# Strassen's scheme for layer 1's last two blocks, and layer 2's weights by way of DRAM scratch

## The chip, the core and the metric

The kernel runs on one core of one Trainium2 chip. The metric is the device time of one execution in microseconds (us); before the change it is 572.56 us, the median of three runs. Five engines work side by side, each through its own instructions in order: TensorE (PE in the profile), VectorE (DVE), ScalarE (ACT), GpSimd (POOL) and SyncE (SP), which issues the DMAs. Between engines there are only semaphores, so an instruction that waits holds up everything behind it on its engine.

## What is computed

A linear-attention pass over 4 batches, 8 heads and 768 positions gives `attn_out`; it is laid out as 3072 tokens of 256 features and goes through two layers of the same shape, all in float32:

```python
x = np.ascontiguousarray(attn_out.transpose(0, 2, 1, 3)).reshape(B * S, H * D)   # 3072 x 256
h = x @ w_in                       # layer 1: 256 -> 2048
g = np.maximum(h, 0.0) + np.log1p(np.exp(-np.abs(h)))
x = (g @ w_out)                    # 2048 -> 256
h = x @ w2_in                      # layer 2
g = np.where(h >= 1, h, np.where(h <= -1, 0.0, (h + 1) ** 2 / 4))
return (g @ w2_out)
```

## The kernel before

The tokens are cut into six blocks of 512 (`c`, 0 to 5), the 2048 features into 16 columns of 128 (`fc`). One **step** is one block and one column in one layer `m`: `up` makes h (128 x 512) in a PSUM bank, an activation makes g, and `down` adds g times the column's rows of `w_out` to the block's two accumulators (`acc`). Float32 products are made of three matmuls: every operand is split into a high part that the matmul takes exactly and a low part that is the rest (`xh`/`xl`, `wih`/`wil`, `woh`/`wol`, `gh`/`gl`), and high x high, high x low and low x high are added. An `up` is 6 matmuls of 512 columns, a `down` 6 too (4 with gh, 2 with gl).

In layer 2 `up` is made by Strassen's scheme: two blocks and two columns form a **quad** of four steps. Instead of 8 products of 3 matmuls it takes 7, of sums of weight pieces (S, made by `s_sum`, `s_hi`, `s_lo`) and sums of token pieces (T, made by `t_sum`, `t_hi`, `t_lo`). On PE a quad is `p15`, `p26`, `p37`, `p4`; between them ACT copies two banks (`fork`, `keep`) and DVE adds twice (`add1`, behind the second product of `p26` and ahead of `p37`; `add2`, behind `p37` and ahead of `p4`). PE fills the gaps with `down` matmuls of earlier steps.

Weights come from HBM as 64-bit numbers. `load_w` brings one eighth of a matrix, `w0` to `w3` turn it into float32 (ACT and DVE), `w_hi` and `split_w` split it. Layer 1's weights are made while the attention of the first blocks runs. Layer 2's take the same SBUF tiles, so each waits for the last use of layer 1's piece (`last_use`); they are made between 230 and 320 us, in three temporaries (`w32`).

The attention of block c, in units of 128 positions per batch, runs between layer 1's steps: loads of `ld`, `u` and `bc` (SP), `decay` scans, `sources`, `weigh` (DVE), `scores`, `st`, `out` (PE), `evac` (ACT) and `ready` (DVE), the last of which gives the block's `xl`.

The order of all this is not written by hand. `program()` lists jobs with engine, cost, needs, buffers taken and given, and due time; `Jobs.order` places them greedily by start time and due time, and the instructions are emitted in that order. `CHUNK` sets how early attention falls due, `LAG` and `LAG_2` how far `down` may follow `up`, `T_POOL` which T sums go to POOL, `STRETCH` how long PE's steps are taken to be.

Of the kernel before, what the change touches and what calls it, by code (L numbers as in the profile page):

```python
# [156 lines left out]
def mlp_steps():  # L157
# [9 lines left out]
    pairs = [(0, NC // 2 - 1)] + [(1, p) for p in range(NC // 2)]  # L167
    steps += [(m, c, 0, T, i, 1) for m, p in pairs for i in range(NFC) for c in (2 * p, 2 * p + 1)]
# [3 lines left out]
def quad_of(s):  # L172

    return s // 4 if s >= NFC * NC else None
# [32 lines left out]
def program():  # L207
# [116 lines left out]
    last_use, first_use = {}, {}  # L324
    for s, (m, c, t0, n, fc, m_fc) in enumerate(steps):
        for j in {(fc + i) // 2 for i in range(m_fc)}:
            last_use[m, "i", j] = ("up", s)
            last_use[m, "o", j] = ("down", s)
            first_use.setdefault((m, j), s)
    for m in range(2):  # L330
        for j in sorted(range(8), key=lambda j: first_use[m, j]):
            for kind in "io":
                w = (m, kind, j)
                add(("load_w", *w), SP, 400, takes=["sx" if m == 0 and j == SX else "st" if m else ("st", "st3")], size=524e3)
                add(
                    ("w0", *w), {ACT: 580} if signed(*w) else {ACT: 580, DVE: 350}, needs=[("load_w", *w)] + [("ready", NU - 1)] * m, takes=["w32"] * m,
                )
                if m < LOW_ACT:
                    add(("w1", *w), ACT, 680, needs=[("load_w", *w)], takes=[("t", "g")])
# [16 lines left out]
    for p in range(NC // 2):
        done = [("finish_lo", 0, c, e) for c in (2 * p, 2 * p + 1) for e in range(2)]
        first = NFC * NC // 4
        late = [[("ready", NU - 1)], [("w3", 1, kind, 7) for kind in "io"] + [("p4", first + 3)], [("p4", first + 9)]][p]
        t = [("t_sum", p, i) for i in range(4)]  # L360
# [137 lines left out]
def tile_kernel(ctx: ExitStack, tc: tile.TileContext, a0, al, bc, ub, w_in, w_out, w2_in, w2_out, out):  # L498
# [894 lines left out]
```

## Time and profile before

| | |
|---|---|
| median of three runs | 572.56 us (572.38 to 572.74) |
| the profiled execution | 571.61 us |
| its span (first to last instruction) | 569.7 us |
| PE busy | 560.1 us (98%) |
| DVE busy | 440.3 us (77%) |
| ACT busy | 335.0 us (59%) |
| POOL busy | 42.3 us (7%) |
| DMA, mean | 68 GB/s |
| granted clock of PE | 0.999 |

The profile is of one execution. Busy is the time in which an engine had an instruction of its own at work. Matmuls overlap in the records: a row says 0.39 us for one, while the next starts 0.227 us later, so times on PE are read from starts. A row's brackets show how long the engine was idle before it and whose signal ended that. A line such as L1176 is a line of the kernel above.

### The profile page before, as it was taken

The numbers are of one execution on the slowest core, as the hardware profiler recorded it, in microseconds if no ns is written. First come the engines' busy times: TensorE is split into PE (matmuls) and PEld (weight loads), VectorE is DVE, ScalarE is ACT, GpSimd is POOL, SyncE is SP. The second block draws the span as 40 slices with busy tenths as digits, with TensorE's granted clock in tenths as the row PEclk, the third lists the DMA queues.
The fourth block names the chain that finished last, engine by engine and source line by source line (L and its number), as shares of the span: only waits on it lengthen the run. The fifth ranks groups of instructions, "written<-read, shape, count | busy, mean of one in ns | idle before, by whom it ended". The sixth has DMA issues, their size and how long they took to land.

```text
span 569.7 us, 10297 instructions
## 1 busy us (share of the span) xinstructions
PE 560.1 (98%) x4103; PEld 450.9 (79%) x4103; DVE 440.3 (77%) x807; ACT 335.0 (59%) x601; POOL 42.3 (7%) x43
## 2 busy tenths in 40 slices
PE   8899999999999999999999999999999999999997
PEld 3778798877877777888888788888887888788885
DVE  7999987647547754799999888977798776876674
ACT  6969343324324322666655877675686764777863
POOL 5230000000000600200020000200021000000000
PEclk9999999999999999999999999999999999999999
DMA  8984653313312200114241000000100000100001
GB/s 275 372 247 156 191 136 105 93 29 104 93 30 75 75 1 2 27 48 145 78 148 37 1 0 1 1 2 0 75 0 2 1 1 37 38 0 2 1 1 74
DMA packets 19988, 38.49 MB, mean 68 GB/s; under 512 B 2052, under 2 KB 2436, under 8 KB 19940
## 3 DMA queue, kind: packets, MB, share of 16 engines
q1 hardware_dynamic: 19940, 37.84, 21.4%
q8 instruction: 32, 0.52, 0.4%
q14 instruction: 16, 0.13, 0.1%
HBM read 34.50 MB, written 3.33 MB: 66 GB/s over the span
## 4 chain that ended last, share of the span: by engine, by line
PE 93%; DVE 2%; DMA 1%; ACT 1%; issue 1%; SPq 1%; DVEq 0%; ACTq 0%
PE acc L1262 44%; PE h L1126 6%; PE h L1127 6%; PE h L1128 6%; PE h L1133 3%; PE h L1135 3%; PE h L1134 3%; PE z L1133 3%; PE z L1135 3%; PE z L1134 3%; PE acc L1250 2%; PE y L1036 1%; DMA st<-in_w_in_dram 1%; PE z L1126 1%; PE z L1127 1%; PE z L1128 1%
## 5 line engine op out<-in xcount | busy, mean ns | idle before, releaser
L1236 DVE TENSOR_TENSOR gl<-g,gh 128x512 fp32r<-128x512 f32 x186 | 130.7, 705 | 36.3 <-PE acc L1262 21.2
L1262 PE MATMUL acc<-gh,woh 128*128 128x512 f32 (+1 forms) x384 | 149.5, 391 | 0.0
L1262 PE MATMUL acc<-gh,wol 128*128 128x512 f32 (+1 forms) x384 | 146.3, 383 | 0.0
L1262 PE MATMUL acc<-gl,woh 128*128 128x512 f32 (+1 forms) x384 | 115.2, 383 | 0.6 <-DVE gl L1236 0.6
L1221 ACT ACTIVATE g<-h 128x512 f32<-128x512 f32 x74 | 44.1, 596 | 105.7 <-PE h L1128 105.0
L623 DVE CAST gh<-g 128x512 fp32r<-128x512 f32 x93 | 42.5, 459 | 55.6 <-ACT g L1221 51.1
L1262 PEld LDWEIGHTS acc<-gh,woh 128*128 128x128 f32 x384 | 72.1, 188 | 16.8 <-issue 1.7
L1262 PEld LDWEIGHTS acc<-gl,woh 128*128 128x128 f32 x384 | 70.8, 188 | 15.3 <-DVE gl L1236 1.0
L1262 PEld LDWEIGHTS acc<-gh,wol 128*128 128x128 f32 x384 | 72.2, 188 | 13.3
L621 ACT CAST gh<-g 128x512 fp32r<-128x512 f32 x93 | 57.7, 620 | 30.9 <-PE acc L1262 20.2
L1126 PE MATMUL h<-xh,wih 128*128 128x512 f32 (+1 forms) x180 | 67.6, 376 | 0.0
L1127 PE MATMUL h<-xh,wil 128*128 128x512 f32 (+1 forms) x180 | 65.9, 366 | 0.0
L1128 PE MATMUL h<-xl,wih 128*128 128x512 f32 (+1 forms) x180 | 65.8, 365 | 0.0
L1213 ACT ACTIVATE t<-t 128x512 f32<-128x512 f32 x96 | 60.8, 634 | 2.2
L1126 PEld LDWEIGHTS h<-xh,wih 128*128 128x128 f32 x180 | 33.9, 188 | 6.2 <-issue 0.5
L1127 PEld LDWEIGHTS h<-xh,wil 128*128 128x128 f32 x180 | 33.9, 189 | 6.0 <-issue 0.5
L1128 PEld LDWEIGHTS h<-xl,wih 128*128 128x128 f32 x180 | 33.9, 188 | 5.7
L1206 ACT ACTIVATE t<-h 128x512 f32<-128x512 f32 x37 | 22.1, 597 | 14.7 <-PE h L1135 11.4
L932 DVE TENSOR_TENSOR_SCAN ld<-ld,eye_t 128x512 f32<-128x512 f32 x20 | 25.7, 1318 | 1.7 <-DMA ld<-clip_z 1.7
L1206 ACT ACTIVATE t<-z 128x512 f32<-128x512 f32 x35 | 20.8, 595 | 9.9 <-PE z L1135 7.7
L1225 DVE TENSOR_TENSOR g<-h,t 128x512 f32<-128x512 f32 x37 | 25.4, 685 | 1.2 <-DVE gl L1236 0.5
L1225 DVE TENSOR_TENSOR g<-z,t 128x512 f32<-128x512 f32 x35 | 23.9, 686 | 0.6
(337 smaller groups left out, 884.7 us busy)
## 6 DMA issues: line engine op xcount, KB each, us to landing
st<-in_w_in_dram SPq DMA_DIRECT2D x15, 512.0 KB, 4.1
st<-in_w_out_dram SPq DMA_DIRECT2D x15, 512.0 KB, 4.3
u<-in_ub_dram SPq DMA_DIRECT2D x24, 256.0 KB, 5.2
ld<-clip_z SPq DMA_DIRECT2D x20, 256.0 KB, 4.4
bc<-in_bc_dram SPq DMA_DIRECT2D x12, 384.0 KB, 3.5
out_dram<-st_plain SPq DMA_DIRECT2D x6, 256.0 KB, 2.0
dec<-clip_p SPq DMA_DIRECT2D x5, 256.0 KB
out_dram<-dec_plain SPq DMA_DIRECT2D x4, 256.0 KB, 2.2
```

The lines of the kernel that those rows point to most:

```text
L621: nc.scalar.copy(out, in_)
L623: engines[engine].tensor_copy(out, in_)
L1126: nc.tensor.matmul(o, wh, xh[c][:, k, t0:t0 + n], start=(k == 0), stop=False)
L1127: nc.tensor.matmul(o, wl, xh[c][:, k, t0:t0 + n], start=False, stop=False)
L1128: nc.tensor.matmul(o, wh, xl[c][:, k, t0:t0 + n], start=False, stop=(k == 1))
L1133: nc.tensor.matmul(bank, wh, bh, start=start, stop=False, skip_group_check=True)
L1206: nc.scalar.activation(out=t, in_=ph, func=act_funcs.IDENTITY_SAT240, scale=SAT)
L1213: nc.scalar.activation(out=t, in_=t, func=AF.Square, scale=0.5 / SAT, bias=0.5)
L1221: nc.scalar.activation(out=g, in_=ph, func=AF.Softplus)
L1225: nc.vector.tensor_tensor(out=g, in0=ph, in1=t, op=ALU.max)
L1236: engines[engine].tensor_tensor(out=mine("g_lo", s)[0], in0=mine("g", s)[0], in1=mine("g_hi", s)[0].bitcast(F32), op=ALU.subtract)
L1262: nc.tensor.matmul(acc_t(s, e), w, g[:, j * n:(j + 1) * n], start=(begins(e, j) and g is gh and i == 0), stop=(fc + j == NFC - 1 and g is ...
```

## The change

Blocks 4 and 5 of layer 1 go by quads as well. So there are four groups of eight quads, in the order of `GROUPS`: layer 1's blocks 4 and 5, then layer 2's blocks 0 and 1, 4 and 5, 2 and 3. Layer 1's S are summed from the split weights that lie in SBUF (`a_sum`, `a_hi`, `a_lo`) once the last whole step has used them.

Layer 2's weights no longer wait for layer 1's tiles. From attention unit 11 on (`PRE_FROM`) they are loaded and made beside layer 1 in five temporaries, split there (`w_hi`, `w_lo`, `s_hi`, `s_lo`), written to DRAM (`put_w`, `put_s`), and read into the tiles by DMA when those are free (`split_w`, `get_s`). Three tiles of blocks 2 and 3 are moved to DRAM (`spill`) so that T of the second group has room, and come back (`fill`). T sums all go to DVE (`T_POOL = ()`), attention falls due sooner (`CHUNK` 8 for 14).

```diff
-    pairs = [(0, NC // 2 - 1)] + [(1, p) for p in range(NC // 2)]
-    steps += [(m, c, 0, T, i, 1) for m, p in pairs for i in range(NFC) for c in (2 * p, 2 * p + 1)]
+    steps += [(m, c, 0, T, i, 1) for m, p in GROUPS for i in range(NFC) for c in (2 * p, 2 * p + 1)]
...
-    return s // 4 if s >= NFC * NC else None
+    return s // 4 if s >= NFC * (NC - 2) else None
...
+                add(
+                    ("load_w", *w), SP, 400, needs=[("ready", PRE_FROM)] * m,
+                    takes=["sx" if m == 0 and j == SX else "st" if m else ("st", "st2", "st3")], size=524e3,
+                )
...
-                add(("w_hi", *w), {ACT: 520, DVE: 350}, needs=[w_made] + ([last_use[0, kind, j]] if m else []))
-                add(("split_w", *w), {DVE: 610, POOL: 1500}, needs=[("w_hi", *w)], gives=[("w0", *w)] * m)
+                add(("w_lo", *w), DVE, 610, needs=[("w_hi", *w)])
+                add(("put_w", *w), SP, 800, needs=[("w_lo", *w)], gives=[("w0", *w)] * (kind == "o"), size=524e3)
+                add(("split_w", *w), SP, 800, needs=[("put_w", *w), last_use[0, kind, j]], size=524e3)
+                if kind == "i":
+                    add(("s_sum", j), DVE, 800, needs=[("w3", *w)])
+                    add(("s_hi", j), {ACT: 420, DVE: 280}, needs=[("s_sum", j), ("put_w", *w)])
+                    add(("s_lo", j), DVE, 470, needs=[("s_hi", j)])
+                    add(("put_s", j), SP, 800, needs=[("s_lo", j)], gives=[("w0", *w)], size=393e3)
+                    add(("get_s", j), SP, 800, needs=[("put_s", j), last_use[0, kind, j]], size=393e3)
...
+    for j in range(8):
+        ours = [("out", 3)] if j < 3 else [("out", NU - 1)]
+        add(("a_sum", j), DVE, 610 + 4 * 210, needs=[("split_w", 0, "i", j), last_whole[j]], takes=["w32"])
+        add(("a_hi", j), {ACT: 900, DVE: 640}, needs=[("a_sum", j), last_whole[j]] + ours)
+        add(("a_lo", j), DVE, 860, needs=[("a_hi", j)], gives=[("a_sum", j)])
...
+    for i in range(3):
+        add(("spill", i), SP, 400, needs=finished(2, 3), size=524e3)
+        last = ("p4", (NFC * NC + 2 * NFC) // 4 - 1)
+        add(("fill", i), SP, 400, needs=[("spill", k) for k in range(3)] + [last], size=524e3)
...
-            ("down", s), PE, down, due=when(s) + (LAG_2 if m else LAG), needs=needs,
+            ("down", s), PE, down, due=when(s) + (LAG if quad_of(s) is None else LAG_2 if m else LAG_1), needs=needs,
...
-    slots = dict(sx=2, h=2, y=1, z=0, acc=4, t=2, g=N_G, gh=4, gl=3, ld=3, lp=2, u=4, bc=3, bt=3, dec=2, st=3, st3=1, w32=3, cs=2)
+    slots = dict(sx=2, h=2, y=1, z=0, acc=4, t=2, g=N_G, gh=4, gl=3, ld=3, lp=2, u=4, bc=3, bt=3, dec=2, st=2, st2=1, st3=1, w32=5, cs=2)
...
-CHUNK = 14
+CHUNK = 8
...
-STRETCH = 1.0
+STRETCH = 1.02
...
+LAG_1 = 6000
...
-T_POOL = 1
+T_POOL = ()
+GROUPS = [(0, 2), (1, 0), (1, 2), (1, 1)]
```

In the whole program PE has 24 matmuls of 512 columns less (504 in `product` and 516 in `up` before, 672 and 324 now), DVE 896 compute instructions for 807, ACT 654 for 598, POOL 34 for 43, SP 216 transfers and branches for 114.

On PE, the first quad of the program before (layer 2, blocks 0 and 1). The z rows with `u0_later` and `u1_later` are the second product of `p26`, the h rows with `xh1` and `xl1` the first of `p37`, which adds onto the bank that `add1` writes:

```order
L1133 MATMUL h0_158<-xh0_302,wih0_73 128x512
L1134 MATMUL h0_158<-xh0_302,wil0_81 128x512
L1135 MATMUL h0_158<-xl0_303,wih0_73 128x512
L1133 MATMUL z0_2830<-u0_later_2881,ld0_later_2962 128x512
L1134 MATMUL z0_2830<-u0_later_2881,ld0_later_2962 128x512
L1135 MATMUL z0_2830<-u1_later_2922,ld0_later_2962 128x512
L1133 MATMUL h1_160<-xh1_872,ld0_later_2962 128x512
L1134 MATMUL h1_160<-xh1_872,ld0_later_2962 128x512
L1135 MATMUL h1_160<-xl1_873,ld0_later_2962 128x512
```

And the first quad now (layer 1, blocks 4 and 5), the same two products:

```order
L1250 MATMUL h0_207<-u0_later_2585,ld0_later_2694 128x512
L1251 MATMUL h0_207<-u0_later_2585,ld0_later_2694 128x512
L1252 MATMUL h0_207<-u1_later_2619,ld0_later_2694 128x512
L1379 MATMUL acc2_281<-gh_3050,woh7_96 128x512
L1379 MATMUL acc2_281<-gh_3050,wol7_104 128x512
L1379 MATMUL acc3_287<-gh_3050,woh7_96 128x512
L1379 MATMUL acc3_287<-gh_3050,wol7_104 128x512
L1379 MATMUL acc2_281<-gl_3058,woh7_96 128x512
L1379 MATMUL acc3_287<-gl_3058,woh7_96 128x512
L1250 MATMUL h1_209<-xh5_2316,ld0_later_2694 128x512
L1251 MATMUL h1_209<-xh5_2316,ld0_later_2694 128x512
L1252 MATMUL h1_209<-xl5_2317,ld0_later_2694 128x512
```

A whole `down` now stands between the two.

On DVE, where the attention of block 4 gives its first `xl4` (`ready`, L1096). Before, it stands among steps of layer 1, without work on weights:

```order
L1236 TENSOR_TENSOR gl_2176<-g_2161,gh_2163 128x512
L1096 TENSOR_TENSOR xl4_2172<-y_211,xh4_2171 128x2x256
L1024 SCALAR_TENSOR_TENSOR s0_66<-s0_66,dec1_134,y_211 128x64 x2
L623 CAST gh_2199<-g_2197 128x512
L1236 TENSOR_TENSOR gl_2207<-g_2197,gh_2199 128x512
```

Now it stands among the making of layer 2's weights, at its second `ready` (L1213). The first row is a `w_lo` (L883), which ends the data of a `put_w` from `st3_plain`; L740, L751 and L758 are `w1` to `w3` of the next weight; the last row is that weight's `w_hi`, which writes into `st3_plain` and so waits for the store's landing:

```order
L883 TENSOR_TENSOR st3_plain_1654<-st3_plain_1654,more0_plain_2002 128x512
L740 TENSOR_SCALAR st2_plain_1566<-st2_plain_1566 128x512
L751 SCALAR_TENSOR_TENSOR st2_plain_1566<-st1_136,st2_plain_1566 128x512
L1213 TENSOR_TENSOR xl4_1954<-y_260,xh4_1953 128x2x256
L1141 SCALAR_TENSOR_TENSOR s1_67<-s1_67,dec1_134,y_260 128x64 x2
L1353 TENSOR_TENSOR gl_2157<-g_2130,gh_2133 128x512
L758 SCALAR_TENSOR_TENSOR st2_plain_1566<-st1_136,st2_plain_1566 128x512
L665 CAST st3_plain_1654<-st2_plain_1566 128x512
```

Between the store's data and the operation that waits for its landing stand one `ready`, two carries, one gl and three steps of the next weight; before, no operation here waited for a DMA of weights.

On SP, the last loads of attention before are followed by loads of weights alone:

```order
L891 DMA u0_129<-in_ub_dram 128x512
L891 DMA u1_130<-in_ub_dram 128x512
L902 DMA ld3_120<-clip_z_149 64x2x512 x2
L891 DMA u2_131<-in_ub_dram 128x512
L891 DMA u3_132<-in_ub_dram 128x512
L668 DMA st2_137<-in_w2_in_dram 128x2x512
L668 DMA st0_135<-in_w2_out_dram 128x2x512
```

Now stores (L888 `put_w`, L787 `put_s`) and loads of the weights stand among them:

```order
L1019 DMA ld4_121<-clip_z_149 64x2x512 x2
L1008 DMA u0_129<-in_ub_dram 128x512
L1008 DMA u1_130<-in_ub_dram 128x512
L710 DMA st1_136<-in_w2_out_dram 128x2x512
L888 DMA pre_i10_152<-more0_plain_2002 128x512
L888 DMA pre_i11_153<-st3_plain_1654 128x512
L1019 DMA ld3_120<-clip_z_149 64x2x512 x2
L1008 DMA u2_131<-in_ub_dram 128x512
L1008 DMA u3_132<-in_ub_dram 128x512
```

Each store waits on SP for the DVE or ACT operation that makes its data, and the attention loads behind it wait with it.

## Rows read from the trace of the kernel before

**Rows 1.** The page: busy us and share of each engine; chain by engine.

```profile
PE 560.1 (98%) x4103; PEld 450.9 (79%) x4103; DVE 440.3 (77%) x807; ACT 335.0 (59%) x601; POOL 42.3 (7%) x43
...
PE 93%; DVE 2%; DMA 1%; ACT 1%; issue 1%; SPq 1%; DVEq 0%; ACTq 0%
```

**Rows 2.** Chain of work that ended last, in order: start us, us, what.

```profile
555.14 10.89 PE acc L1262 x48
```

**Rows 3.** PE's waits: line <- releaser: us in total, times, longest.

```profile
PE z L1133 <- DVE z L1176: 1.3, 2, 0.9
...
PE h L1133 <- DVE h L1176: 0.8, 1, 0.8
...
PE acc L1262 <- DVE gl L1236: 0.6, 1, 0.6
```

**Rows 4.** Timeline at 320 and 485 us: start, us, instruction [idle <- releaser].

```profile
320.01 0.39 PE L1135 MATMUL z<-u_later,ld_later 128*128 128x512 f32 x1
...
320.44 0.70 DVE L1176 TENSOR_TENSOR h<-z,dec_plain 128x512 f32<-128x512 f32 x1
...
321.19 0.50 PE L1133 MATMUL h<-xh,ld_later 128*128 128x512 f32 x1 [0.79 <-DVE h L1176]
...
485.57 0.39 PE L1135 MATMUL h<-u_later,ld_later 128*128 128x512 f32 x1
...
486.82 0.50 PE L1133 MATMUL z<-xh,ld_later 128*128 128x512 f32 x1 [0.86 <-DVE z L1176]
```

**Rows 5.** Timeline at 193 to 199 us and 427 to 432 us.

```profile
192.96 4.48 DVE L932 TENSOR_TENSOR_SCAN ld<-ld,eye_t 128x512 f32<-128x512 f32 x2
...
194.26 2.10 POOL L746 TENSOR_TENSOR dec_plain<-st_plain,dec_plain 128x512 f32<-128x512 f32 x1
...
197.37 1.71 DVE L1236 TENSOR_TENSOR gl<-g,gh 128x512 fp32r<-128x512 f32 x1
...
199.13 0.73 PE L1262 MATMUL acc<-gl,woh 128*128 128x512 f32 x2 [0.56 <-DVE gl L1236]
...
427.01 0.68 DVE L1225 TENSOR_TENSOR g<-dec_plain,t 128x512 f32<-128x512 f32 x1
...
427.22 1.62 POOL L771 TENSOR_TENSOR more_later<-more_plain,eye_later 128x512 fp32r<-128x512 f32 x1 [2.01 <-ACT eye_later L621]
...
427.61 1.86 DVE L623 CAST gh<-g 128x512 fp32r<-128x512 f32 x2
...
431.93 0.50 PE L1133 MATMUL z<-xh,ld_later 128*128 128x512 f32 x1 [0.40 <-DVE z L1176]
```

**Rows 6.** Groups of instructions on DVE: xcount | busy us, mean ns | idle before.

```profile
L1236 DVE TENSOR_TENSOR gl<-g,gh 128x512 fp32r<-128x512 f32 x186 | 130.7, 705 | 36.3 <-PE acc L1262 21.2 <-ACT gh L621 9.7 <-ACT t L1206 1.5
...
L623 DVE CAST gh<-g 128x512 fp32r<-128x512 f32 x93 | 42.5, 459 | 55.6 <-ACT g L1221 51.1 <-PE acc L1262 3.4
...
L1186 DVE TENSOR_TENSOR more_plain<-h,more_plain 128x512 f32<-128x512 f32 x7 | 4.8, 691 | 2.8 <-PE h L1135 2.8
...
L698 DVE TENSOR_SCALAR st_plain<-st_plain 128x512 uint32<-128x512 uint32 x11 | 4.6, 421 | 0.0
...
L1096 DVE TENSOR_TENSOR xl<-y,xh 128x256 fp32r<-128x256 f32 x4 | 1.7, 422 | 1.0 <-ACT s L1090 1.0
...
L726 DVE TENSOR_TENSOR dec_plain<-dec_plain 128x128 f32<-128x128 f32 x6 | 1.7, 291 | 0.1
```

**Rows 7.** Busy us (count) of each engine in two stretches; clock, DMA share, GB/s.

```profile
105.00:240.00 135.00, 134.44 (x1471) 105.99 (x1469) 83.76 (x166) 48.81 (x93) 10.69 (x7) 1.00 0.16 45
240.00:315.00 75.00, 75.00 (x332) 62.15 (x331) 68.78 (x140) 43.09 (x76) 5.28 (x6) 1.00 0.29 92
```

**Rows 8.** DMA issues: KB, us to landing; issue time ns min/median/max.

```profile
st<-in_w_in_dram SPq DMA_DIRECT2D x15, 512.0 KB, 4.1
...
out_dram<-st_plain SPq DMA_DIRECT2D x6, 256.0 KB, 2.0
...
L866 SPq DMA_DIRECT2D out_dram<-st_plain x6: 332/367/425, 401.4 to 566.0; - x6
```

More of the change, by code (lines that the diff above doesn't have):

```diff
@@ L356, in program @@
[L356 to L360, printed above, removed]
-        sums = lambda n: {POOL: 1400 * n} if p < T_POOL else {DVE: 610 * n}
-        add(t[0], sums(4), needs=done + late, takes=[("cs", "w32")] * 3)
+                add(("w_hi", *w), {ACT: 520, DVE: 350}, needs=[w_made])
@@ L363, in program @@
+    for k, (m, p) in enumerate(GROUPS):
+        done = finished(2 * p, 2 * p + 1) if m else [("ready", NU - 1)]
+        done += [
+            [], [("spill", i) for i in range(3)], [("p4", NFC * NC // 4 - 1)],
+            [("fill", i) for i in range(3)],
+        ][k]
+        t = [("t_sum", k, i) for i in range(4)]
+        sums = lambda n: {POOL: 1400 * n} if k in T_POOL else {DVE: 610 * n}
+        add(t[0], sums(4), needs=done, takes=["w32"] * 3)
         add(t[2], sums(1), needs=[t[0]])
@@ L379, in program @@
             needs = [("finish_lo", 0, c, e) for e in range(2)]
-        needs += [("split_w", m, "i", j) for j in pieces] + [("up", s - 1)] * m
+        needs += [("split_w", m, "i", j) for j in pieces]
         up, down = pe_time(s)
@@ L384, in program @@
         made, frees = ("up", s), ("up", s)
-        if m == 0:
+        if quad_of(s) is None:
             add(("up", s), PE, up, due=when(s), needs=needs, takes=[bank])
@@ L408, in program @@
             add(
-                ("g", s), ACT, 500 if s else 1850, needs=[("up", s)] + [("decay", b, hg) for b in range(NB * (s == 0)) for hg in range(2)]
+                ("g", s), ACT, 500 if s else 1850, needs=[made] + [("decay", b, hg) for b in range(NB * (s == 0)) for hg in range(2)]
                 + [("w0", 0, kind, j) for kind in "io" for j in range(8 * (s == 0)) if signed(0, kind, j)],
-                takes=["gh" if whole(s) else "g"], gives=[("up", s)],
+                takes=["gh" if whole(s) else "g"], gives=[frees],
             )
@@ L471 @@
 LOW_ACT = 1
+PRE_FROM = 11
 BIAS = {DVE: 0, POOL: 2000}
@@ L728, in s_hi, with put_s @@
     @job
     def s_hi(engine, j):
-        copy(engine, s_all(j, 0), temp("s_sum", j)[0][:, 0:384])
+        w, hi = s_pre(j)
+        copy(engine, hi.bitcast(F32R), w)
     @job
     def s_lo(engine, j):
-        hi, lo = (s_all(j, k) for k in range(2))
-        engines[engine].tensor_tensor(out=lo, in0=temp("s_sum", j)[0][:, 0:384], in1=hi.bitcast(F32), op=ALU.subtract)
+        w, hi = s_pre(j)
+        nc.vector.tensor_tensor(out=w.bitcast(F32R), in0=w, in1=hi, op=ALU.subtract)
+    @job
+    def put_s(engine, j):
+        for lo, t in enumerate(reversed(s_pre(j))):
+            nc.sync.dma_start(pre_s[j, lo], t)
@@ new lines, in a_parts, with a_hi, a_lo @@
+    def a_parts(j, lo):
+        t, (s2, s3, s4, s1) = a_blocks(j)
+        s = s_all(j, lo)
+        return (s[:, 0:128], s2), (s[:, 128:384], t[:, 256:512]), (s_of(j, 2, lo), s3)
+    @job
+    def a_hi(engine, j):
+        for out_, in_ in a_parts(j, 0):
+            copy(engine, out_, in_)
+    @job
+    def a_lo(engine, j):
+        for (lo, in_), (hi, _) in zip(a_parts(j, 1), a_parts(j, 0)):
+            nc.vector.tensor_tensor(out=lo, in0=in_, in1=hi.bitcast(F32), op=ALU.subtract)
+    @job
```

122 lines of the change are left out of this document (89 added, 33 removed).

## The prediction

> **What bounds the kernel now.** I read the page's busy shares and the chain of work that ended last first. TensorE is busy 98% of the span and carries 93% of the chain; VectorE has 77%, and the chain stands on it for 2% [rows 1]. Then the chain's pieces in order of time, for what a matmul costs there: 48 in a row take 10.89 us, so 0.227 us each, without a gap [rows 2]. So behind the first 30 us every matmul less is 0.227 us less, as long as whatever feeds TensorE keeps up. Then TensorE's waits, for what it has lost besides: behind its start only four waits count, two on z and one on h written at L1176 and one on gl written at L1236, 2.7 us in all [rows 3]. The timeline shows what each of them is.
>
> At 320 and 485 us it is the program's order: the second half of p26 ends, add1 (L1176, 0.70 us) can only start then, and the next thing in TensorE's order is p37, which needs add1. From 320.01 to 321.19 is one matmul and a hole of 0.95 us; from 485.57 to 486.82 of 1.02 us [rows 4]. At 199 and 432 us it is GpSimd. While L746 runs there, two scans take 4.48 us and a gl takes 1.71 us; while L771 runs there, two casts of g take 1.86 us [rows 5], where one gl is 0.705 and one such cast 0.459 us in the mean [rows 6]. TensorE waits 0.56 and 0.40 us behind these.
>
> Last, the windows: from 105 to 240 us VectorE is busy 83.8 of 135 us, from 240 to 315 us 68.8 of 75 us, and in that second stretch TensorE is busy 75.00 of 75 [rows 7]. So a VectorE at 92% starves nobody here, provided the order suits it.
>
> **The change part by part.** *Matmuls.* Blocks 4 and 5 of layer 1 have 8 column pairs. Each pair took 8 products of 3 matmuls and now takes 7: 24 matmuls less, 24 x 0.227 = **5.4 us off the path** [rows 2]. Nothing is added on TensorE.
>
> *The order of TensorE.* In all 32 quads of the new order at least six down matmuls (6 x 0.227 = 1.36 us) stand between the second half of p26 and p37; before, quads 0 and 16 had none. What add1 needs between them is read at 320 us: from 320.24 (320.01 + 0.227) to 321.19, 0.95 us [rows 4]. So the holes of 0.95 and 1.02 us close. What is late next is add2 before p4, where six or twelve matmuls stood before too and no wait shows.
>
> *GpSimd.* The T sums leave it (T_POOL is empty). Of its 18 operations of sums and splits behind 100 us it keeps six. The pair L743/L746 at 199 us, the cause of that wait, is gone. The one at 432 us was behind a split of T, of which five remain. I count both old waits as gone (0.56 + 0.40) and price the new ones from them below. With the 0.16 us by which a hole at 320 us is longer than its idle time (0.95 against 0.79), the four are worth 0.95 + 1.02 + 0.72 + 0.56 = **3.3 us**.
>
> *VectorE, more work.* Counted in both orders, with the means of [rows 6]: 16 more add1/add2, 16 x 0.69 = 11.0; a_sum 8 x 0.69 + 32 x 0.29 = 14.8; a_lo 16 x 0.29 + 8 x 0.42 = 8.0; T sums 16 x 0.69 = 11.0 (half of them from GpSimd) and 5 splits of T 3.4; s_sum, w0 and the rest 0.8; 17 casts go to ScalarE, 17 x 0.46 = -7.8. Sum 41 us. ScalarE takes 16 fork/keep and some twenty casts, which it has room for (59% busy). If all 41 us fell between 105 and 315 us, VectorE would have 83.8 + 68.8 + 41 = 193.6 of 210 us: 92%, what it stands at now between 240 and 315 us with TensorE at 75.00 of 75 [rows 7]. And the old hump is levelled, since layer 2's weights are made from 100 us on instead of behind 230 us. So I cost it at nothing on average; only where attention, weights and quads fall together (140 to 180 us by the order) can it bite. Bounds: 0, and 2.7 us (all the waits TensorE has on VectorE now, once more [rows 3]). I take 0.5.
>
> *The way through DRAM.* 16 weights and 8 sums are written to scratch, two stores each, and read back, by the order, 40 us or more before their use; so the reads (32 + 16 loads) are hidden. The stores matter because the temporaries are few: five slots, reused as soon as a store has landed, and a VectorE operation that waits for it holds all behind it, the gl among them, which TensorE waits for. One of the shortest trips in the order has w1, w2, ready, two carries, a gl and w3 between the w_lo that ends the store's data and the CAST that waits for it (the DVE rows of the change): 0.42 + 2 x 0.69 + 0.69 + 2 x 0.29 + 0.705 = 3.8 us by the means; neighbours start 0.60 us apart where the mean is 0.69 [rows 5], so I reckon with 3.1. Some seven others have up to 5 us; the other 16 have more. A store of 256 KB here lands 2.0 us after its issue, and an issue takes 0.37 us [rows 8]: two of them 2.0 + 2 x 0.37 = 2.7 us, inside 3.1. At the other end, if a store took what a load of weights takes (4.1 us), a trip would be 4.8 us, 1.7 us late, eight times 13.6 us. A load is twice the size, so the store's row is the nearest; below nothing is excluded, as these waits are new. I take 0.6.
> The Trainium skill (DMA: Bandwidth & Descriptors, Anatomy of one DMA) speaks against such trips: most of a transfer's fixed 2 us is the receipt from the target memory, and with HBM as target this can be surprisingly long. Its fit gives an estimate of 2.0 + 0.6 = 2.6 us for 256 KB, 3.3 us with the issues, which leaves the sum as it is; only a longer receipt would make the rival below.
>
> *SyncE's queue.* It gets 102 more transfers, at 0.37 us 38 us of issue over 300 us. Attention's loads of ld and u now stand behind stores that wait for VectorE. Before, weight loads that wait for w3 stood ahead of them likewise. Cost nothing; bounds 0 and 0.56 us (the wait at 199 us behind the scans, the only one of its kind). I take 0.3.
>
> *GpSimd's rest and the layers' border.* Six operations, of 18 that cost 0.96 us of TensorE's idle time: 6/18 x 0.96 = 0.3 (0 to 1). The border, where ScalarE evicts four banks between two layers, and the fourth group's start: 0.3 (0 to the 0.95 of an old start).
>
> *Sum.* New waits 0.5 + 0.6 + 0.3 + 0.3 + 0.3 = 2.0 us. -5.4 - 3.3 + 2.0 = **-6.7 us**. The profiled execution took 571.61 us with a span of 569.7, so span 563.0 and time 564.9; the median of the three runs is 0.95 us higher than that execution, 572.56, so **565.9 us**.
>
> **The rivals.** *Everything hides* (no new wait at all): 572.56 - 8.7 = 563.9 us. For it: slack in every place I counted. Against: a new order of 800 VectorE operations with 24 new trips; the old one had four waits.
> *Only the matmuls are gained, or less*: new waits of 3.3 to 7 us, the price of the old four or twice that, 567.2 to 571.2 us. The place: the stretch from 140 to 180 us, where VectorE has scans, weights and gl in a row, and the first quad, where a_lo, w_lo and w0 to w3 stand between two gl and add1.
> *Slower*: the stores land late. One mechanism: VectorE waits at the eight short trips. At 1.7 us each 13.6 us, 572.56 - 8.7 + 13.6 = 577.5 us. It decides from 8.7 / 8 = 1.1 us a trip on, that is a landing of 3.1 - 0.74 + 1.1 = 3.5 us instead of 2.0. Against it: six stores on the same queue at 2.0 to 2.3 us [rows 8]; for it: loads at 4.1 us, and stores now share the engines with loads.
> *The matmuls are not the bound.* TensorE's busy share is modelled, and if the feed were the limit, 24 matmuls less would bring nothing: 572.56 - 3.3 + 2.0 = 571.3 us, at the edge of no change. Against it stand 48 matmuls in 10.89 us without a gap. The Trainium skill (Trace Analysis, Identifying the Most-Contended Engine) says to judge TensorE by weight loads rather than by matmul time; those are busy 79% here, which by that rule is headroom, but the chain shows the rows back to back.
>
> **How the numbers follow.** A measurement of this kernel tells 0.2% (1.1 us) from no change. Forecast with everything hidden or nearly (563.5 to 567.2): 0.6. Only the matmuls or less (567.2 to 571.4): 0.22. Within 0.2% (the feed binds, or new waits eat about nine us): 0.06. Slower: 0.12. The range from 563.4 to 570.8 leaves out the slower cases and the last piece of the second. Faster 0.82, same 0.06, slower 0.12.
>
> **What would show it.** Right: 672 matmuls of products and 324 of up; TensorE idle at most 2 to 3 us behind 30 us, no hole ahead of p37 in any quad, no wait behind GpSimd at the T sums; VectorE near 440 + 41 = 481 us busy and spread evenly. Wrong: waits of VectorE on stores (st_plain and more_plain ahead of a CAST or a w1) with TensorE's waits on gl behind them; a stretch from 140 to 180 us with TensorE below 98%; waits of p37 at the first quad of layer 1. If the span falls by less than 5.4 us, new waits outweigh the old ones, and the step that failed is the 2.0.

## The result, and the profile after

| | before | after |
|---|---|---|
| median, us | 572.56 (3 runs), 572.74 (5 runs beside after) | 566.18 (5 runs, 564.84 to 567.62) |
| profiled execution, us (span) | 571.61 (569.7) | 566.18 (564.5) |
| ratio after / before | | 0.9881, 95% interval 0.9860 to 0.9902 |

Predicted were 565.9 us, with 563.4 to 570.8 as the range. The time came out 0.3 us above that; whether it did so for the reasons given is what the runs below are for. One trace below, that of the run with 24 matmuls put back, is from an execution at a mean granted clock of 0.853 (622.17 us), and is not read.

The page of after, the lines that answer to [rows 1] (busy us and share of each engine; the chain by engine):

```profile
PE 554.8 (98%) x4079; PEld 446.1 (79%) x4079; DVE 469.8 (83%) x896; ACT 358.4 (63%) x657; POOL 30.0 (5%) x34
...
PE 86%; DVE 5%; DMA 4%; ACT 2%; issue 1%; SPq 1%; DVEq 0%; ACTq 0%
```

The last piece of its chain in order of time (start us, us, what), the answer to [rows 2]:

```profile
550.91 9.53 PE acc L1379 x42
```

TensorE has 24 matmuls less (4103 to 4079) and is still busy 98% of the span; a matmul still takes 9.53 / 42 = 0.227 us. VectorE and ScalarE have gained about 30 and 23 us, GpSimd has lost 12.

TensorE's waits, all of them (line <- releaser: us in total, times, longest), the answer to [rows 3]:

```profile
PE y L1093 <- DMA bc<-in_bc_dram: 1.8, 1, 1.8
PE y L1456 <- DVE xl L1213: 1.3, 1, 1.3
PE h L1410 <- DVE idle L1408: 1.1, 1, 1.1
PE z L1250 <- ACT h L1278: 0.6, 1, 0.6
PE h L1250 <- DVE dec_plain L1303: 0.4, 1, 0.4
PE y L1185 <- ACT sm L1222: 0.2, 1, 0.2
```

The first three belong to the start. Behind it none of the four old waits is left: no wait on add1 (L1293), none on a gl (L1353). Two larger new ones stand there: on ScalarE's `fork` (L1278) and on VectorE's `add2` (L1303). I measure a hole from the start of one matmul to the start of the next, less 0.227 us, and count those over 0.13 us behind 45 us. Before has 0.95 + 1.02 + 0.72 + 0.56 = 3.26 us of them (the four of [rows 4, 5]). After has 0.72 at 403, 0.60 at 278, 0.25 at 321 and 0.16 at 319 us, 1.73 us in the quads, and 0.22 us at 65 us in attention (the last line above), 1.95 in all. The timeline shows the two large ones (start, us, instruction [idle <- releaser]):

```profile
277.06 0.69 DVE L883 TENSOR_TENSOR st_plain<-st_plain 128x512 fp32r<-128x512 f32 x1
...
277.67 0.68 DVE L1303 TENSOR_TENSOR dec_plain<-h,dec_plain 128x512 f32<-128x512 f32 x1
...
278.41 0.50 PE L1250 MATMUL h<-eye_later,wih 128*128 128x512 f32 x1 [0.43 <-DVE dec_plain L1303]
...
401.25 1.30 POOL L868 TENSOR_TENSOR xh_later<-st_plain,xh_later 128x512 fp32r<-128x512 f32 x1 [57.37 <-ACT xh_later L663]
...
401.63 1.46 DVE L868 TENSOR_TENSOR xl_later<-st_plain,xl_later 128x512 fp32r<-128x512 f32 x1
...
403.02 0.68 DVE L1342 TENSOR_TENSOR g<-h,t 128x512 f32<-128x512 f32 x1
...
403.46 0.39 PE L1252 MATMUL h<-more_later,wih 128*128 128x512 f32 x1
...
403.79 0.57 ACT L1278 COPY h<-z 128x512 f32<-128x512 f32 x1 [0.74 <-DVE g L1342]
...
404.41 0.50 PE L1250 MATMUL z<-xh,wih 128*128 128x512 f32 x1 [0.56 <-ACT h L1278]
```

At 278 us a `w_lo` (L883), work for layer 2 that nobody needs yet, stands ahead of add2 on VectorE. At 403 us GpSimd makes one split of T beside VectorE, whose own takes 1.46 us instead of 0.69; the g behind it frees a bank late, and ScalarE's fork, which writes into that bank, holds p26. The small hole at 65 us begins with a scan that waited for its load:

```profile
61.80 2.34 DVE L1049 TENSOR_TENSOR_SCAN ld<-ld,eye_t 128x512 f32<-128x512 f32 x2 [2.19 <-DMA ld<-clip_z]
...
65.18 0.58 PE L1185 MATMUL y<-u,sm 32*64 32x64 f32 x24 [0.23 <-ACT sm L1222]
```

The windows that answer to [rows 7], and the stretch that the prediction feared (busy us and count of PE, PEld, DVE, ACT, POOL; clock, DMA share, GB/s):

```profile
105.00:240.00 135.00, 135.00 (x1384) 106.88 (x1384) 120.67 (x270) 77.85 (x156) 1.62 (x1) 1.00 0.39 129
240.00:315.00 75.00, 74.56 (x328) 60.99 (x327) 62.03 (x116) 42.94 (x73) 1.61 (x1) 1.00 0.75 246
140.00:180.00 40.00, 40.00 (x529) 31.18 (x528) 34.83 (x73) 20.23 (x39) 0.41 (x1) 1.00 0.39 133
```

VectorE is level now, 89 and 83% of the two stretches instead of 62 and 92%, and TensorE is without a gap from 105 to 240 us in this execution (not in every one, see the next section). The groups that answer to [rows 6]:

```profile
L1353 DVE TENSOR_TENSOR gl<-g,gh 128x512 fp32r<-128x512 f32 x185 | 128.0, 695 | 31.9 <-PE acc L1379 20.8 <-ACT t L1323 5.2 <-ACT gh L663 3.0
L665 DVE CAST gh<-g 128x512 fp32r<-128x512 f32 x75 | 31.5, 424 | 13.4 <-ACT g L1338 8.9 <-PE acc L1379 3.3
```

The transfers that answer to [rows 8] (KB each, median us from issue to landing):

```profile
st<-in_w_in_dram SPq DMA_DIRECT2D x15, 512.0 KB, 6.3
...
pre_o<-st_plain SPq DMA_DIRECT2D x15, 256.0 KB, 3.3
pre_i<-st_plain SPq DMA_DIRECT2D x13, 256.0 KB, 4.2
...
out_dram<-st_plain SPq DMA_DIRECT2D x7, 256.0 KB, 2.0
```

A store to the output still lands after 2.0 us; the stores to scratch, beside loads, after 3.3 and 4.2.

### The profile page after: what moved, and what is told of

Read it like the earlier page. It is cut to its first block, busy times and chain, and to the rows that moved or that the text cites. A ratio compares the mean times of both kernels' runs of the same rounds, so it can differ in the third digit from the quotient of the medians.

```text
span 564.5 us, 10573 instructions
## 1 busy us (share of the span) xinstructions
PE 554.8 (98%) x4079; PEld 446.1 (79%) x4079; DVE 469.8 (83%) x896; ACT 358.4 (63%) x657; POOL 30.0 (5%) x34
## 4 chain that ended last, share of the span: by engine, by line
PE 86%; DVE 5%; DMA 4%; ACT 2%; issue 1%; SPq 1%; DVEq 0%; ACTq 0%
PE acc L1379 42%; PE h L1250 4%; PE h L1251 4%; PE h L1243 4%; PE h L1252 4%; PE h L1244 4%; PE h L1245 4%; PE z L1250 4%; PE z L1251 4%; PE z L1252 4%; PE acc L1367 2%; PE y L1153 1%; DMA st<-in_w_in_dram 1%; DMA ld<-clip_z 1%; PE y L1185 1%
## 5 line engine op out<-in xcount | busy, mean ns | idle before, releaser
L1353 DVE TENSOR_TENSOR gl<-g,gh 128x512 fp32r<-128x512 f32 x185 | 128.0, 695 | 31.9 <-PE acc L1379 20.8
L663 ACT CAST gh<-g 128x512 fp32r<-128x512 f32 x111 | 68.9, 621 | 29.8 <-PE acc L1379 20.1
L1338 ACT ACTIVATE g<-h 128x512 f32<-128x512 f32 x63 | 37.5, 595 | 59.3 <-PE h L1245 40.7
L1243 PE MATMUL h<-xh,wih 128*128 128x512 f32 (+1 forms) x126 | 47.6, 378 | 0.0
L1244 PE MATMUL h<-xh,wil 128*128 128x512 f32 (+1 forms) x126 | 45.0, 357 | 0.0
L1245 PE MATMUL h<-xl,wih 128*128 128x512 f32 (+1 forms) x126 | 44.8, 356 | 0.0
L665 DVE CAST gh<-g 128x512 fp32r<-128x512 f32 x75 | 31.5, 424 | 13.4 <-ACT g L1338 8.9
L1243 PEld LDWEIGHTS h<-xh,wih 128*128 128x128 f32 x126 | 23.8, 189 | 5.1 <-issue 1.2
L1244 PEld LDWEIGHTS h<-xh,wil 128*128 128x128 f32 x126 | 23.8, 189 | 3.5 <-issue 0.5
L1245 PEld LDWEIGHTS h<-xl,wih 128*128 128x128 f32 x126 | 23.8, 189 | 3.6
L1303 DVE TENSOR_TENSOR dec_plain<-h,dec_plain 128x512 f32<-128x512 f32 x24 | 16.5, 688 | 9.8 <-PE h L1252 9.6
```

The costliest lines, as they stand in the source:

```text
L663: nc.scalar.copy(out, in_)
L1243: nc.tensor.matmul(o, wh, xh[c][:, k, t0:t0 + n], start=(k == 0), stop=False)
L1244: nc.tensor.matmul(o, wl, xh[c][:, k, t0:t0 + n], start=False, stop=False)
L1245: nc.tensor.matmul(o, wh, xl[c][:, k, t0:t0 + n], start=False, stop=(k == 1))
L1338: nc.scalar.activation(out=g, in_=ph, func=AF.Softplus)
L1353: engines[engine].tensor_tensor(out=mine("g_lo", s)[0], in0=mine("g", s)[0], in1=mine("g_hi", s)[0].bitcast(F32), op=ALU.subtract)
```

## The experiments

Each run stands beside runs of the kernel before on the same chip, whose medians were 572.7 to 573.3 us.

**The changed kernel again.** 

> The changed kernel as it is, once more, as the yardstick for the kernels that run beside it. Theory (its gain is in the program's order): ratio to the kernel before 0.988 again, a span of 563 to 565 us, and the same two holes of TensorE, 0.95 us at about 403 us and 0.82 us at about 278 us from start to start of two matmuls. Rival (the holes are chance of one execution): a hole of the same length at other places, or none.

Measured: 566.77 us (565.76 to 568.91), ratio 0.9892 (0.9872 to 0.9911). The hole behind the split is there again, 0.72 us at 405. The one at add2 is 0.15 us this time, and 0.47 to 0.61 us in three other executions. This profile has one more hole, 0.71 us at 130 us, inside a group of attention's products, where the profile shows nothing that TensorE waited for:

```profile
PE y L1153 <- issue: 0.7, 1, 0.7
```

Five other profiles of kernels that make layer 2's weights early have it too, 0.29 to 1.04 us between 127 and 132 us; the profile of the result and that of the kernel with both repairs below do not, nor do the five of the kernel before and its variants. What causes it is open. With it the holes behind 45 us are 2.56 us here.

**24 matmuls put back.**

```diff
-        product(mine("fork", q)[0], w(1, 1), t(3), False)
+        for _ in range(1 + (group_of(q) == 0)):
+            product(mine("fork", q)[0], w(1, 1), t(3), False)
```

> The changed kernel, with each product of p4 made twice in the eight quads of layer 1, so that the 24 matmuls that Strassen's scheme saves there are on TensorE again (the sum is wrong by one product). Nothing else moves. Theory (TensorE is the bound, 0.227 us a matmul): 24 x 0.227 = 5.4 us slower than the changed kernel, 571.6 us. Rival (what feeds TensorE is the bound): no slower than the changed kernel by more than 1 us, since VectorE, ScalarE and the transfers do what they did.

Measured: 571.73 us, ratio 0.9981 (0.9970 to 0.9993). That is 5.0 us behind the changed kernel beside it (566.77), 0.207 us a matmul, with an uncertainty of about 1.3 us in the 5.0: TensorE is the bound. What feeds it was not touched, and does not set the time.

**GpSimd's five splits of T to VectorE.**

```diff
     def t_lo(engine, p, i):
-        engines[engine].tensor_tensor(out=t_of(p, i, 1), ...)
+        nc.vector.tensor_tensor(out=t_of(p, i, 1), ...)
```

> The changed kernel, with the five splits of T (L868) that GpSimd makes given to VectorE at the same place of the program. Theory (the hole at 403 us comes from GpSimd: its L868 runs from 401.25 us beside one on VectorE, which takes 1.46 instead of 0.69 us, and the g behind that, ScalarE's fork and p26 are late by as much): that hole closes from 0.95 to 0.23 us, 0.7 us faster than the changed kernel, 565.4 us; the hole at 278 us stays. Rival (VectorE is too full for five more operations of 0.69 us, or the fork is late for another reason): the hole stays, or new ones open at the other four places, 0 to 2 us slower.

Measured: 565.91 us, ratio 0.9879 (0.9864 to 0.9895), 0.9 us under the changed kernel beside it. The same place in its timeline:

```profile
403.25 0.68 DVE L1342 TENSOR_TENSOR g<-h,t 128x512 f32<-128x512 f32 x1
...
404.02 0.57 ACT L1278 COPY h<-z 128x512 f32<-128x512 f32 x1
...
404.70 0.44 PE L1250 MATMUL z<-xh,wih 128*128 128x512 f32 x1
```

The hole is gone; one of 0.25 us stands 3 us later, where add1 is behind the added split. That shows what made the hole. That the kernel is faster by it is not shown: the intervals of the two kernels overlap.

**And add2 ahead of the w_lo.**

```diff
+        names = [o[0] for o in order]
+        order.insert(names.index(("w_lo", 1, "o", 4)), order.pop(names.index(("add2", 20))))
+        names = [o[0] for o in order]
```

> As the kernel with the splits on VectorE, and besides the operation add2 of the fifth quad of layer 1's... of the fifth quad in the order is moved ahead of the w_lo (L883) that stood before it on VectorE. Theory (the hole at 278 us is add2 waiting for 0.7 us of weight work that nobody needs yet): that hole closes too, 0.6 us more, 1.3 us faster than the changed kernel in all, 564.9 us. Rival (add2 is late because p37 is, or VectorE's lateness only moves to the next gl): no faster than with the splits alone, and a wait on gl of about 0.6 us behind 278 us.

Measured: 565.69 us (565.67 to 567.11), ratio 0.9877 (0.9860 to 0.9893). Neither large hole is left, and no wait on a gl follows behind 278 us. This is the fastest of all kernels here by its median, 1.1 us under the changed kernel beside it, though again within the intervals.

**Stores that hold no temporary.**

```diff
-            nc.sync.dma_start(pre_s[j, lo], t)
+            nc.sync.dma_start(pre_s[j, lo], flat(wt["o", "l", 7])[:, 0:384].bitcast(F32))
...
-            nc.sync.dma_start(pre_w[kind, j, lo], t)
+            nc.sync.dma_start(pre_w[kind, j, lo], flat(wt["o", "l", 7]).bitcast(F32))
```

> The changed kernel, with the 48 stores to scratch made from a weight tile that nobody rewrites till late, instead of from the temporaries; as many stores and loads of the same size (layer 2 computes with the wrong weights). No operation has to wait for a store any more before it writes a temporary. Theory (the waits for stores fall on ScalarE, 2.6 us in two places, and TensorE never sees them): the same time as the changed kernel within 0.5 us, and ScalarE's two waits gone. Rival by the prediction's step (VectorE is held by them, 0.6 us): 0.6 us faster. Rival (stores that land after 3.3 to 4.2 us cost 8 trips x 1 us): several us faster.

Measured: 566.23 us, ratio 0.9891 (0.9870 to 0.9913): the same as the changed kernel (0.9892 beside its own runs of before). As many stores and loads run, but no operation waits for a store. ScalarE's two waits for stores, here of the changed kernel, are gone in it:

```profile
ACT more_plain L663 <- DMA pre_i<-more_plain: 2.2, 1, 2.2
...
ACT st_plain L726 <- DMA pre_o<-st_plain: 0.4, 1, 0.4
```

VectorE has no wait for a store in either, and TensorE keeps its two large holes (0.47 us at 278, 0.72 at 403). So waiting for the trips costs nothing that shows, with an uncertainty of about 1.7 us in the times; where a trip did end late, ScalarE took it.

**Every store twice.**

```diff
...
-            nc.sync.dma_start(pre_w[kind, j, lo], t)
+            for copies in (again_w, pre_w):
+                nc.sync.dma_start(copies[kind, j, lo], t)
```

The stores of the S sums (`put_s`) are doubled in the same way.

> The changed kernel, with each of the 48 stores to scratch made twice, the first time to a second scratch that nobody reads: each trip is two issues longer, 2 x 0.37 = 0.74 us, and 11 MB more are written. Theory (trips have slack on VectorE, and ScalarE takes the short ones): less than 1 us slower than the changed kernel, ScalarE's waits for stores longer by some 2 to 4 us in all, VectorE's still under 2. Rival (the short trips are at their limit already, since the stores land after 3.3 to 4.2 us): 8 x 0.74 = 5.9 us slower, with waits of VectorE for stores and of TensorE on gl behind them.

Measured: 573.72 us, ratio 1.0015 (1.0000 to 1.0030), 7 us behind the changed kernel. My theory fell. ScalarE's waits for stores, and the waits of TensorE that follow, in its profile:

```profile
ACT st_plain L728 <- DMA pre_o<-st_plain: 6.8, 3, 3.1
...
ACT more_plain L665 <- DMA pre_i<-more_plain: 2.3, 1, 2.3
```

```profile
PE z L1254 <- ACT h L1282: 2.1, 2, 1.6
PE h L1254 <- DVE dec_plain L1307: 2.0, 1, 2.0
...
PE acc L1383 <- DVE gl L1357: 1.1, 2, 0.9
```

And one of these places in its timeline:

```profile
305.22 0.66 ACT L728 ACTIVATE st_plain<-st 128x512 f32<-128x512 f32 x1 [3.09 <-DMA pre_o<-st_plain]
...
305.78 0.58 ACT L1282 COPY h<-z 128x512 f32<-128x512 f32 x1
...
306.41 0.50 PE L1254 MATMUL z<-xh,wih 128*128 128x512 f32 x1 [1.58 <-ACT h L1282]
```

A `w0` on ScalarE (L728) waits 3.09 us for the store; the fork of the next quad is queued behind it, and p26 behind that. The largest hole, 2.17 us at 323 us ahead of a product that waits for add2, follows another such wait: the w0 at 318.72 us had waited 2.53 us, and behind it come ScalarE's load of the next activation's table, the first g of layer 2, and VectorE's evictions and add2. Another hole, 1.1 us ahead of a gl at 292 us, follows a w0 on VectorE that waited 2.97 us for a transfer; whether for its own load or for a store, the profile's name for it doesn't settle. The new holes stand between 285 and 330 us, at the last trips; from 140 to 240 us TensorE is busy 100.00 of 100 as in the changed kernel. So the rival's mechanism is real and its size (5.9 us) about right, but it needs 0.74 us more a trip and longer landings (4.3 and 6.0 us here), it bites mostly through ScalarE, and only at the last weights. Some 1.6 of the 7 us are a lower clock behind the hole at 323 us (last section).

**The kernel before, with work put between p26 and p37.** First try:

```diff
+        names = [o[0] for o in order]
+        for q, s in ((24, 94), (40, 157)):
+            order.insert(names.index(("down", s)), order.pop(names.index(("p15", q))))
+            names = [o[0] for o in order]
+        for q, s in ((24, 95), (40, 159)):
+            order.insert(names.index(("p26", q)), order.pop(names.index(("down", s))))
+            names = [o[0] for o in order]
```

The first loop puts p15 ahead of a down, the second puts another down behind p26.

> The kernel before, with TensorE's order changed at two quads only (the first of layer 2's first and third pair of blocks): p15 goes ahead of the down that stood before it, and the down that stood before p26 goes behind it, so that six down matmuls stand between p26's second half and p37. Theory (the holes of 0.95 us at 320 and 1.02 us at 485 us are the order alone): both close, 2.0 us faster than the kernel before, 571.2 us beside 573.2. Rival (add1's or another chain is late there anyway, and the hole moves to p26 or p4): 0 to 0.5 us faster, with a new hole in the same quads.

Measured: 576.69 us, ratio 1.0066 (1.0045 to 1.0087), slower. Six down matmuls do stand ahead of p37 now, and the hole is longer:

```profile
323.44 0.69 DVE L623 CAST xh<-acc 128x512 fp32r<-128x512 f32 x1 [2.77 <-PE acc L1262]
...
324.65 0.69 DVE L1176 TENSOR_TENSOR h<-z,dec_plain 128x512 f32<-128x512 f32 x1
...
325.39 0.50 PE L1133 MATMUL h<-xh,ld_later 128*128 128x512 f32 x1 [1.99 <-DVE h L1176]
```

The down that I moved is the layer's last; VectorE's eviction of its bank (L623) stands ahead of add1 (L1176) and waited for it. The edit made its own wait, and says nothing yet on the old one. The second try moves ScalarE's fork and keep, and VectorE's add1, along:

```diff
...
+        for q, start, s in ((24, ("up", 95), 95), (40, ("down", 158), 159)):
+            put(("p15", q), start)
+            put(("fork", q), ("p15", q))
+            put(("keep", q), ("fork", q))
+            put(("down", s), ("p26", q))
+            put(("add1", q), ("p26", q))
```

Here `put(a, b)` moves a to the place behind b.

> The kernel before with TensorE's order changed at the same two quads as in the first try, and with ScalarE's fork and keep moved up behind p15 and VectorE's add1 moved up ahead of the eviction of the layer's last banks, on which it stood waiting in the first try. Theory (the holes at 320 and 485 us are the program's order on three engines): both close but for 0.2 us, 1.5 to 2.0 us faster than the kernel before, 570.7 to 571.2 beside 572.7. Rival (at these two places, between two layers and between two pairs of blocks, there is no work to put there, and the hole only moves): 0 to 0.5 us faster, or slower, with a hole within 5 us of the old ones.

Measured: 573.71 us, ratio 1.0015 (1.0001 to 1.0029): no gain. At 485 us the hole shrinks from 1.02 to 0.46 + 0.26 us, at 320 from 0.95 to 0.45, but 1.80 us open at 323:

```profile
322.22 1.28 ACT L1206 ACT_TABLE_LOAD   x1
323.51 0.60 ACT L1206 ACTIVATE t<-h 128x512 f32<-128x512 f32 x1
...
324.80 0.69 DVE L1225 TENSOR_TENSOR g<-h,t 128x512 f32<-128x512 f32 x1 [0.91 <-ACT t L1213]
...
325.55 0.50 PE L1133 MATMUL h<-xh,ld_later 128*128 128x512 f32 x1 [1.63 <-DVE g L1225]
```

Between the layers ScalarE loads a table for the other activation (1.28 us), then works on the first g of layer 2, which VectorE ends (L1225), and TensorE waits for the bank which that g frees. A down taken from there is missing there: the rival was right, the hole moves.

**The kernel before, with GpSimd's sums and splits of T on VectorE.**

```diff
+            if engine == POOL and name[0] in ("t_sum", "t_hi", "t_lo"):
+                engine = ACT if name[0] == "t_hi" else DVE
```

> The kernel before, with the sums and splits of T that GpSimd makes (four sums, six splits) given to VectorE at the same places of the program. Theory (VectorE was slow at 199 and 432 us because GpSimd worked beside it): the holes of 0.72 and 0.56 us there close, 1.3 us faster than the kernel before, 571.9 beside 573.2. Rival (ten pieces more of 0.69 us each on VectorE hold gl and add1 as much as GpSimd did): no faster, with holes at other places within 5 us of the old ones.

Measured: 571.41 us, ratio 0.9980 (0.9966 to 0.9994): 1.1 us faster (0.3 to 1.9), as expected within its uncertainty. The hole at 199 us is gone, that at 432 us is 0.28 instead of 0.56 us; those at 320 and 485 us stay to the hundredth.

**Both edits of before in one.** 

> Both edits of the kernel before in one: the order at two quads, and GpSimd's sums and splits of T on VectorE. Theory (four old stalls, 3.3 us, are worth what the prediction said, and are got without Strassen's scheme in layer 1): 569.4 beside 572.7 us, ratio 0.994; what the changed kernel gains beyond that, 3.3 us, is 24 matmuls less its new waits. Rival (the stalls are no loss that adds up: what follows them is held by something else): 571 to 572 us.

Measured: 572.50 us, ratio 0.9995 (0.9981 to 1.0008). The 3.3 us are not to be had in the old kernel: what GpSimd gives, the border takes back (1.81 us at 325 us again).

**Strassen's scheme undone in layer 1, all else of the change kept.**

```diff
 def quad_of(s):
-    return s // 4 if s >= NFC * (NC - 2) else None
+    return s // 4 if s >= NFC * NC else None
...
-    for j in range(8):
+    for j in range(0):
         ours = [("out", 3)] if j < 3 else [("out", NU - 1)]
...
     for k, (m, p) in enumerate(GROUPS):
+        if m == 0:
+            continue
...
-            [], [("spill", i) for i in range(3)], [("p4", NFC * NC // 4 - 1)],
+            [], [("spill", i) for i in range(3)], [("up", NFC * NC - 1)],
...
-                needs += [("add1", q - 1)] * (s > NFC * (NC - 2))
+                needs += [("add1", q - 1)] * (s > NFC * NC)
```

> The changed kernel with Strassen's scheme undone in layer 1's last two blocks alone: 24 more matmuls, no a_sum, no T sums and no add1/add2 for them; the weights of layer 2 still go through scratch, no T sum is on GpSimd, and the planner's numbers are those of the changed kernel. In its order one of the two old places (the first quad of layer 2) has nothing between p26 and p37. Theory (the way through scratch costs TensorE nothing by itself, and gains nothing): 566.5 + 5.4 + 0.95 less the waits that the layer-1 quads had (0.6 to 0.9 us), 572 us, as the kernel before. Rival (most of the change's gain is the planner's new order and the weights that are made early): 567 to 569 us. Rival (the way through scratch costs several us, hidden by nothing here): 574 us and more.

Measured: 574.32 us, ratio 1.0018 (1.0004 to 1.0032), 2 us over the expectation. Beside the old 0.95 us at 320 a hole of 1.87 us opens at 324, behind add2:

```profile
323.59 1.28 DVE L842 TENSOR_TENSOR st_plain<-xh,xl 128x512 f32<-128x512 f32 x2
...
326.12 0.68 DVE L1305 TENSOR_TENSOR dec_plain<-h,dec_plain 128x512 f32<-128x512 f32 x1
...
326.86 0.50 PE L1252 MATMUL h<-xh_later,wih 128*128 128x512 f32 x1 [1.71 <-DVE dec_plain L1305]
```

These are T sums of layer 2, which the line with `("up", NFC * NC - 1)` released some ten us too early. With `("p4", NFC * NC // 4 + 2)` in its place:

> As the kernel with Strassen's scheme undone in layer 1's last two blocks, but the T sums of layer 2's second pair of blocks, which stood between two quads at the layers' border there (2.6 us of VectorE ahead of add2, and a hole of 1.87 us of TensorE), come some ten us later, where the changed kernel has them. Theory (that hole was those sums, and what is left is the old border): the hole of 0.95 us at 320 us stays, those of 1.87 and 0.50 us behind it close to under 0.5 us together, 572.3 us, and so 5.7 to 6.2 us behind the changed kernel: 24 matmuls (5.4), the border (0.95 less the 0.41 us that the changed kernel has there). Rival (without Strassen's scheme the border has no work to spare, and a stall of about 3 us stands there whatever is moved): 574 us again, the holes at other matmuls within 15 us of the border.

Measured: 571.75 us, ratio 0.9983 (0.9971 to 0.9996). Behind 100 us it has three holes: the old one at the border (0.95 us), the one behind GpSimd's split (0.72 us) and the unexplained one at 131 us (0.58 us).

So the parts are: the way through scratch, the new order and the T sums off GpSimd together 1.0 us by the ratio (0.2 to 1.7) and 1.5 us by the medians (573.28 to 571.75), Strassen's scheme in layer 1 another 5.0 to 5.6 us (571.75 to 566.77 or 566.18). Within the first part the planner's numbers were not tried one by one.

## Why the prediction was right, step by step

- **Matmuls, -5.4: right.** 24 fewer in the profile, 0.227 us each in the chain; 5.0 us when they are put back, 5.0 to 5.6 when the scheme is undone (which also opens and closes other holes). The rival that they are not the bound is out.
  The Trainium skill (Perfetto Trace Analysis, Identifying the Most-Contended Engine) judges TensorE's headroom by the share of peak arithmetic and by weight loads. By weight loads alone, 79% busy here, there would have been headroom, and the 24 matmuls show that there was none.
- **GpSimd, -1.28: right.** The same move in the kernel before gains 1.1 us and closes one hole and half of the other.
- **Order, -2.0: right in the outcome, wrong in its reason.** I counted what stands between p26 and p37, found six down matmuls, and called the holes closed. In the kernel before six were put there and nothing was gained. At the border the work itself is short: evictions of four banks, a table load and the first g of layer 2 all come at once. In the changed kernel layer 1's last blocks are quads too, and by its timeline p4 of the old layer and three downs stand between p15 and p37 of the new one (310.5 to 316.6 us). Without the scheme in layer 1 the 0.95 us is back at the same planner's numbers. So about 0.5 us (0.95 less the 0.41 at 319 and 321 us) of what I gave to the order comes with Strassen's scheme. The other hole, at 485 us, is gone with and without it; which part of the new order closed it, no run shows.
- **VectorE's load, 0.5: size right, place wrong.** 0.60 + 0.16 us, at 278 and 319 us, behind weight work and evictions; at 140 to 180 us, which I named, TensorE is busy 40.00 of 40. VectorE is 469.8 us busy and not 481: I had used the means of before, which held GpSimd's disturbance. With GpSimd's T work on VectorE the kernel before has 0.428 us a cast of g instead of 0.459. In the changed kernel the casts of g alone fell by 11.0 us where I took 7.8 off, since 75 of them take 0.424 us now, and 185 gl cost 2.7 us less; that is about half of the 11 us, the rest I did not trace.
- **Trips through scratch, 0.6: nothing was lost, and two of its rows were wrong.** I took a landing of 2.0 us, from stores that had the transfers to themselves; among loads they land after 3.3 to 4.2. By my own threshold (3.5) the 4.2 should have decided for the slower rival. It did not, because the short trip was longer than I reckoned (w_lo ends at 142.28 us and the cast behind the wait starts at 146.06, 3.8 us and not 3.1), one of its two stores is issued 8 us earlier (134.06 us), and the two trips that did end on a landing (2.2 and 0.4 us) have ScalarE as the next writer, and TensorE did not wait behind it. That the kernel was not slower is in this term luck. The doubled stores show how near the edge is: 7 us.
  On the receipt the Trainium skill (DMA: Bandwidth & Descriptors, Anatomy of one DMA) was nearer than my row: it warns that with HBM as target it can be long. The estimate of 2.6 us for 256 KB, worked out from its fit for DMAs that GpSimd issues, is exceeded by 0.7 to 1.6 us by these stores, which SyncE issues.
- **SyncE's queue, 0.3: 0.22 us, but not by the stores.** Attention's loads land later (6.9 us for ld<-clip_z, 4.4 before), and VectorE's scans wait 3.2 us for them in all (1.7 before). The longest of these waits, 2.19 us at 61.80 us, leads to the hole of 0.22 us at 65 us; its load was on its way from 55 us on, and the first store to scratch is issued at 111 us.
- **GpSimd's rest, 0.3: 0.72 us, mis-sized.** Five of its six operations cost nothing, one met VectorE's split ahead of a fork. A collision costs all or nothing, and its share of a mean was no price.
- **Border and fourth group, 0.3: 0.25 us**, at 321 us.

The short trip of the stores, from the changed kernel's timeline (its w_lo, and the cast that waits for the landing):

```profile
141.60 0.68 DVE L883 TENSOR_TENSOR st_plain<-st_plain,more_plain 128x512 fp32r<-128x512 f32 x1
...
146.06 0.43 DVE L665 CAST st_plain<-st_plain 128x512 fp32r<-128x512 f32 x1
```

The new waits were 2.0 us by the prediction and 1.95 us by the trace; that they agree so well is partly luck, as 0.6 too much for the trips stands against 0.7 too little for GpSimd and VectorE. One bound in the prediction is misreckoned: new waits of 7 us give 572.56 - 8.7 + 7 = 570.9 us, not 571.2 or 571.4; nothing hangs on it.

The span fell by only 5.2 us, and the prediction had said that under 5.4 the new waits would outweigh the old. That sign was badly chosen. The matmuls and holes counted here make 5.4 + 1.3 = 6.7 us. Of the missing 1.5 us, 0.5 lie ahead of the first product of 512 columns (it starts at 31.65 and 32.18 us, and anywhere between 31.1 and 33.4 us in thirteen profiles of these kernels), about 0.35 behind the start of the last matmul (4.08 and 4.43 us to the end of the span), and the rest in gaps below 0.13 us and ahead of 45 us. The holes, counted behind the start, were the thing to look at.

## What to carry to other kernels

Count the holes of the bounding engine matmul by matmul on both sides, and leave the start out: that gave 1.3 us here where the span could not. Leave out enough of it: two profiles of variants of the kernel before have 2.0 and 2.4 us of holes between 45 and 57 us, ahead of everything that their edits touch. At the border of the two layers the hole closed where work of the old phase was left over, and not where the little that was there was shifted; try the shift in the old kernel before crediting the order. When temporaries go to DRAM, ask which engine writes the temporary next and what is queued behind that write, and measure the margin by doubling the stores, since no cost that shows and 7 us lay 0.74 us of issue and 1 to 2 us of landing a trip apart.

## What the hardware showed besides

A store of 256 KB to scratch landed after a median of 3.3 to 4.2 us in a stretch with 130 to 250 GB/s on the transfers, and after 2.0 us where it had them to itself.

With the stores doubled, TensorE's clock fell for some 3 us, behind holes of 1.7 us at 304 and 2.2 us at 323 us, the two largest (windows: busy us and count of PE, PEld, DVE, ACT, POOL; granted clock, DMA share, GB/s):

```profile
324.00:328.00 4.00, 2.26 (x8) 1.85 (x9) 4.00 (x8) 3.54 (x7) 0.00 (x0) 0.87 0.46 170
328.00:332.00 4.00, 4.00 (x14) 3.19 (x13) 2.81 (x7) 2.89 (x6) 0.00 (x0) 0.70 0.02 6
```

Its timeline there:

```profile
328.72 0.63 PE L1254 MATMUL z<-xh,wih 128*128 128x512 f32 x1
...
329.15 0.63 PE L1255 MATMUL z<-xh,wil 128*128 128x512 f32 x1
```

Eight matmuls between 327.0 and 330.4 us are 0.43 us apart instead of 0.23, the lower of the two clock levels (1.2 GHz instead of 2.4), which adds some 1.6 us to the 2.2 us of the hole at 323. The mean granted clock is 0.996 or 0.997 in eleven of the twelve executions of this kernel, and 1.000 in the fastest (572.02 us); where it fell is known for the profiled one alone, and 0.996 occurs in some executions of the kernel before too. In the first shifted kernel a hole of 2.15 us at the same place, behind one of 1.6 us, had no such fall in the profile (granted clock 1.00 from 324 to 332 us), so what makes the clock fall is left open.
